# Attention maxima over 64 queries of two heads and 320 keys, with the attention's operands held in rings of chunks

## The chip, the cores and the metric

The kernel runs on one core of a Trainium2 chip. The metric is the device time of one execution in microseconds. The core's engines work side by side: TensorE (PE in the profile, its weight loads PEld) multiplies, VectorE (DVE), ScalarE (ACT) and GpSimd (POOL) do elementwise work, and SyncE (SP) issues the transfers (DMAs). Each engine executes its own instructions in a fixed order, and semaphores hold an instruction until what it needs is there.

## The reference

A gated mix of sliding-window attention and a two-layer gelu network, all in float32, over 2048 tokens of width 512; the attention has 32 heads of 16, each query sees itself and the 255 keys before it, and the inner width of the network is 1792.

```
qkv = (x @ wqkv).reshape(B, S, 3, H, Dh)
scores = einsum("bhqd,bhkd->bhqk", q, k) * Dh ** -0.5
mask = (idx[:, None] - idx[None, :] >= 0) & (idx[:, None] - idx[None, :] < W)
p = softmax(where(mask, scores, -1e9))
a = einsum("bhqk,bhkd->bhqd", p, v) ... @ wo
b = gelu(x @ w1 + b1) @ w2 + b2
g = sigmoid((x * gate_w).sum(-1))
return g * a + (1 - g) * b
```

## The kernel before

**Arithmetic.** Dense products are made of three matmuls each (`mm3`, L89 to L92): every operand is split into a high and a low part, and high by high, high by low and low by high are added in PSUM. The scores carry the split in their contraction instead: for one head the 16 elements of `q` and `k` stand there with high and low parts, 48 rows in all, so that two heads fill 96 of the 128 partitions.

**Stages.** Four tiles of 512 tokens are projected first (`qkv`): `q`, `k` and `v` go out to DRAM as `SQ`, `SK` and `SV`. The attention then runs over 8 groups of four heads, and in each over 16 blocks of 128 keys: 128 units `u`. Four units of one group (512 tokens) are called a chunk here; there are 32. The network (`mlp`) and the last product with `wo` (`final`) are cut into pieces of a few matmuls and put between the attention's by `fill`, so that TensorE has dense work while the attention's other engines run.

**The attention.** For a unit the maxima come first, 8 units ahead of the rest (LEAD):
- `att_max` (L385): a matmul `sm` (L394) gives the scores of 128 queries of one head by 384 keys; a reduction on DVE (L399) adds the mask and puts the maxima into `M`. Four of these per unit, one for each head.
- `att_rows` (L405): once a chunk, the negated maxima in two parts are transposed on DVE (`tt`, L414) and copied by four casts on POOL (L419) into eight further rows (96 to 103) of `qs`. The matching rows of `ks` hold ones for their own head (`clear_k`), so that the next matmul subtracts the maximum by itself.
- `att_exp` (L425): a matmul `st` (L435) gives, for 64 keys of two heads, the scores of 320 queries, transposed; ACT takes the exponential into `pt` (L450), and POOL zeroes the two corners outside the window (L441, L444).
- `att_pvs` (L456): once a chunk the products with `vbuf` (L472) collect numerators and denominators in two PSUM tiles; ACT and DVE add them into `nd` (L493, L496), and it is stored as `ND` (L497). For every second group `att_norm` (L503) divides, by way of DRAM (`den`, `RD`, `num`, `rb`, `OT`).

**What holds the operands.** `ks` holds the 2048 keys of one group in the layout that `st` wants: 64 keys of head 0 beside 64 of head 1, with zeros in the other's rows. `sm` reads the same tile with a strided view (`of_head`). `qs` holds the queries for both. `load_k` (L348) and `att_load` (L367) fetch a chunk's keys and queries for a later unit, overwriting those of the group before.

**What sets the order.** The code is unrolled. On PE, ACT, DVE and POOL the order is the one in which the program emits instructions (`manual_schedule`): the main loop, L743 to L774, goes through the units, in each four times through the letters of ORDER (`m` maxima, `s` exponentials, `p` products, `f` dense work of STEP = 2296 ns by the planner's count for a whole unit), and `after` puts follow-up work at a due time on a planner's clock. SP's order comes from the framework's own scheduler. SP issues every DMA of the kernel, in that order: one that waits holds all behind it. Each issue also waits until the DMA eight earlier has landed, since there are eight completion semaphores (DMAHW0 to DMAHW7 in the order).

## Time and profile before

| | us |
|---|---|
| median of 3 runs | 769.8 (769.8 to 769.93) |
| the profiled execution | 769.51 |
| its span, first to last instruction | 767.8 |
| granted TensorE clock, mean | 1.000 |

The profile is one execution. Busy times are sums over an engine's instructions; PE's matmuls overlap in the records, so the distance from start to start tells what one costs. A row of a group of instructions gives line, engine, operation, output and inputs with their shapes, count, busy time, mean ns of one, and the idle time just before them with what ended it. SPq is SP's issuing of DMAs. The page's rows by fortieths of the span show the load of TensorE and of the DMA engines in tenths:

```profile
PE   8999999988999999999999999999999999999998
DMA  9986856765643565575345756653575474436583
```

The first 160 us are projections, with heavy traffic to DRAM; from about 185 to 689 us the attention and the network run side by side; the last 80 us are the network's end and the product with `wo`.

### The profile page before, as it was taken

To read this page: it belongs to the slowest core of one execution; us is meant where nothing else is said; L and a number is where in the kernel's file an instruction comes from. 1 tells how busy PE (TensorE), PEld (TensorE's weight loads), DVE (VectorE), ACT (ScalarE), POOL (GpSimd) and SP (SyncE) were. 2 spreads that over 40 slices of the span, in tenths; PEclk is the share of its full clock that TensorE was granted. 3 is DMA by queue.
4 is the path that set the end of the run, shared out by engine and by line. 5 is a ranking of instruction groups with operands and counts; after the bars stand their busy time and mean duration, and the time that the engine had idled before them with its cause. 6 is when DMAs were issued, how large, how long until landed. Compare 5 with 4: busy or idle time off the path is not lost.

```text
span 767.8 us, 18330 instructions
## 1 busy us (share of the span) xinstructions
PE 748.8 (98%) x6102; PEld 614.3 (80%) x6102; DVE 534.1 (70%) x1548; ACT 432.6 (56%) x945; POOL 385.9 (50%) x1125
## 2 busy tenths in 40 slices
PE   8999999988999999999999999999999999999998
PEld 6888888866888888788877877888888788878786
DVE  4532332889669868976897798679878886893553
ACT  4434433358458646754885587448646763785641
POOL 2200000018666765766567677658765775777200
PEclk9999999999999999999999999999999999999999
DMA  9986856765643565575345756653575474436583
GB/s 299 358 296 203 319 182 219 252 195 166 179 119 73 181 196 138 142 209 151 95 114 156 212 163 193 185 126 94 172 206 158 107 214 125 132 107 200 171 261 110
DMA packets 136558, 137.81 MB, mean 179 GB/s; under 512 B 53264, under 2 KB 88592, under 8 KB 136464
## 3 DMA queue, kind: packets, MB, share of 16 engines
q1 hardware_dynamic: 136464, 136.64, 59.4%
q8 instruction: 49, 0.80, 0.4%
q14 instruction: 45, 0.37, 0.2%
HBM read 82.58 MB, written 54.00 MB: 178 GB/s over the span
## 4 chain that ended last, share of the span: by engine, by line
PE 84%; DVE 8%; issue 3%; ACT 3%; DMA 1%; SPq 1%; POOL 0%; DVEq 0%; POOLq 0%; ACTq 0%
PE sm L394 10%; PE st L435 8%; PE pv_sm L472 7%; PE y L90 7%; PE y L91 6%; PE y L92 6%; PE u L90 5%; PE u L91 5%; PE u L92 5%; PE qk L92 4%; DVE jm L399 4%; PE qk L90 4%; PE qk L91 4%; PE a L90 2%; PE v L92 2%
## 5 line engine op out<-in xcount | busy, mean ns | idle before, releaser
L399 DVE CUSTOM_DVE_ANT_0 jm<-sm,mask 128x384 bf16<-128x384 f32 (+2 forms) x512 | 269.6, 527 | 66.8 <-PE sm L394 38.8
L450 ACT ACTIVATE pt<-st 128x320 f32<-128x320 f32 (+4 forms) x512 | 206.1, 421 | 134.1 <-PE st L435 129.4
L441 POOL TENSOR_SCALAR_AFFINE_SELECT pt<-pt 64x128 f32<-64x128 f32 x512 | 176.5, 345 | 184.8 <-ACT pt L450 166.1
L394 PE MATMUL sm<-ks,qs 96*128 96x384 f32 (+2 forms) x512 | 171.7, 338 | 10.7 <-DVE M L399 9.0
L435 PE MATMUL st<-qs,ks 128*128 128x320 f32 (+4 forms) x512 | 155.0, 305 | 0.7 <-ACT pt L450 0.7
L444 POOL TENSOR_SCALAR_AFFINE_SELECT pt<-pt 64x128 f32<-64x128 f32 x448 | 154.7, 345 | 0.0
L394 PEld LDWEIGHTS sm<-ks,qs 96*128 96x128 f32 x512 | 96.2, 188 | 44.1 <-DVE M L399 21.1
L435 PEld LDWEIGHTS st<-qs,ks 128*128 128x128 f32 x512 | 97.3, 190 | 18.3 <-ACT pt L450 1.1
L90 PE MATMUL y<-w,h 128*128 128x512 f32 x224 | 90.1, 402 | 0.0
L91 PE MATMUL y<-w,h 128*128 128x512 f32 x224 | 88.4, 395 | 0.0
L92 PE MATMUL y<-w,h 128*128 128x512 f32 x224 | 87.8, 392 | 0.0
L419 POOL CAST qs<-tt 8x256 fp32r<-8x256 f32 x128 | 62.3, 487 | 47.2 <-PE u L92 37.9
L90 PE MATMUL u<-mx,w 128*128 128x512 f32 x196 | 80.4, 410 | 0.0
L91 PE MATMUL u<-mx,w 128*128 128x512 f32 x196 | 77.3, 395 | 0.0
L92 PE MATMUL u<-mx,w 128*128 128x512 f32 x196 | 76.8, 392 | 0.0
L472 PE MATMUL pv_st<-pt,vbuf 64*32 64x320 f32 (+4 forms) x1408 | 73.1, 346 | 0.8 <-POOL pt L441 0.8
L472 PE MATMUL pv_sm<-pt,vbuf 64*32 64x320 f32 (+4 forms) x1408 | 73.4, 346 | 0.1
L472 PEld LDWEIGHTS pv_sm<-pt,vbuf 64*32 64x32 f32 x1408 | 49.9, 106 | 19.9 <-issue 2.1
L251 DVE TENSOR_TENSOR qke<-qk,qke 128x512 fp32r<-128x512 f32 x32 | 22.1, 690 | 48.9 <-ACT qke L248 40.5
L248 ACT ACTIVATE qke<-qk 128x512 fp32r<-128x512 f32 x32 | 19.1, 598 | 56.0 <-PE qk L92 37.1
L92 PEld LDWEIGHTS y<-w,h 128*128 128x128 f32 x224 | 42.1, 188 | 9.7
L496 DVE TENSOR_TENSOR nd<-nd,pv_sm 128x512 f32<-128x512 f32 x32 | 21.9, 684 | 39.0 <-ACT nd L493 38.8
(124 smaller groups left out, 1337.6 us busy)
## 6 DMA issues: line engine op xcount, KB each, us to landing
mx<-XT SPq DMA_DIRECT2D x24, 512.0 KB
SQ<-qke SPq DMA_DIRECT2D x16, 512.0 KB
SK<-qke SPq DMA_DIRECT2D x16, 512.0 KB
qs<-SQ SPq DMA_DIRECT2D x32, 256.0 KB
ND<-nd SPq DMA_DIRECT2D x32, 256.0 KB
ks<-SK SPq DMA_DIRECT2D x112, 64.0 KB
raw_w<-in_B_w_dram SPq DMA_DIRECT2D x28, 256.0 KB
SV<-vx SPq DMA_DIRECT2D x16, 272.0 KB
```

The source lines that it names most:

```text
L90: nc.tensor.matmul(p, lh, rh, start=first, stop=False)
L91: nc.tensor.matmul(p, lh, rl, start=False, stop=False)
L92: nc.tensor.matmul(p, ll, rh, start=False, stop=last)
L251: nc.vector.tensor_sub(e[:, 1 - h], p, f32(e[:, h]))
L394: nc.tensor.matmul(p[:, :w], qs[0:96, pr, b * 128:(b + 1) * 128], of_head(ks[0:96, pr, 2 * k0:2 * (k0 + w)], s), start=True, stop=True)
L399: nc.vector.tensor_tensor_reduce(junk[:, :w], p[:, :w], mask[:, 384 - w:384], 1.0, -3e38, ALU.add, ALU.max, M[:, b % RB, i:i + 1])
L419: nc.gpsimd.tensor_copy(dst, tt[32 * i:32 * i + 8].unsqueeze(1).broadcast_to([8, 2, RB, 32]))
L435: nc.tensor.matmul(p[:, :w], ks[:, pr, 2 * k0:2 * k0 + 128], qs[:, pr, k0:k0 + w], start=True, stop=True)
L441: nc.gpsimd.affine_select(out=v[:, :, 0:64], in_=v[:, :, 0:64], pattern=[[0, 2], [1, 64]], compare_op=ALU.is_ge, fill=0.0, base=0, channel ...
L444: nc.gpsimd.affine_select(out=v[:, :, W:W + 64], in_=v[:, :, W:W + 64], pattern=[[0, 2], [-1, 64]], compare_op=ALU.is_ge, fill=0.0, base=- ...
L450: nc.scalar.activation(pt[:, pr, :w], p[:, :w], AF.Exp, scale=SCALE)
L472: nc.tensor.matmul(pv[r // 64][32 * i:32 * i + 32, q - c * T:e - c * T], vts[g_, b // NB][r:r + 64, v:v + 32], rhs(r), start=start, stop=s ...
```

## The change

The maxima get operands of their own, and all of the attention's operands are held by chunks.

- **`sm`** now takes 64 queries of both heads (128 columns of `qd`, 64 of one head beside 64 of the other) by 320 keys (`kd`). The mask has 320 columns, with one 64 by 64 corner pair in each half of the partitions. There are still four `sm` per unit: two halves of the block by two pairs of heads.
- **Heads.** A group is two heads out of each of two 128-wide pieces of the projection, so `SQ` and `SK` in DRAM are laid out by piece, and `SK` is cut into four tiles of 512 tokens.
- **Rings.** `ks`, `qd` and `kd` each have two slots of one chunk; `kd` holds 256 earlier keys besides the 512 (the halo). The slot is the parity of the chunk's number. `qs` keeps all 2048 queries; the rows for the maxima are now 0 to 3 and 64 to 67.
- **Loads.** A chunk takes 6 DMAs for `ks`, 4 for `kd` (2 in a group's first chunk), 4 for `qd` and 4 for `qs`, against 7 to 10 for `ks` and 2 for `qs` before. They are emitted at fixed units: `qd` and `kd` when the maxima begin a chunk, `ks` one unit later, `qs` two units later. SP issues 1029 DMAs in all, 841 before.
- **Maxima's rows.** The transpose is 256 columns wide instead of 128, and each of the four casts writes 4 rows of 2 x 256 elements instead of 8 rows of 2 x 128.
- **Memory.** `pt` has 14 buffers instead of 16, `h` 7 instead of 8, `raw` 2 instead of 3 (early weights use `pt` buffers). The `v` eviction has four pieces instead of two; `wo` comes in four DMAs a block, in the new order of heads; the network's results for the last stage are fetched into `qd` and `kd` instead of `ks`.

```diff
-    SK = dr.tile([H, 16, 2, S], F32, name="SK")
+    SK = [dr.tile([H // NC, 16, 2, NC, T], F32, name=f"SK{t}") for t in range(NT)]
...
-    ks = cp.tile([128, 2, 2 * S], F32R, name="ks")
+    ks = cp.tile([128, 2, 2, 2 * T], F32R, name="ks")
+    qd = cp.tile([128, 2, 2, 2 * T], F32R, name="qd")
+    kd = cp.tile([128, 2, 2, W + T], F32R, name="kd")
...
-            to = vx[:, :, 0:16].rearrange("p (g s a) d -> p g a s d", s=2, a=2)
-            for s in range(2):
+            to = vx[:, :, 0:16].rearrange("p (i g s a) d -> p i s g a d", i=2, s=2, a=2)
...
+    def slot(g_, c):
+        return (g_ * NT + c) % 2
...
+    def parts(st, g_, h):
+
+        for s in range(2):
+            src = heads(st, g_)[s]
+            yield s, 0, 32, src.rearrange("d u a c -> (d u) a c")
+            yield s, 32, 16, src[:, h]
+
+    def load_ks(g_, c):
...
+        for s, r, n, src in parts(SK[c], g_, 0):
+            r += 64 * s + 4
+            v = f32(ks[r:r + n, slot(g_, c)]).rearrange("r a (n u j) -> r (a n) u j", u=4, j=64)
+            src = src.rearrange("r a (n u j) -> r (a n) u j", u=2, j=64)
+            if s:
+                nc.sync.dma_start(v[:, :, 0], src[:, :, 0])
+                nc.sync.dma_start(v[:, :, 3], src[:, :, 1])
+            else:
+                nc.sync.dma_start(v[:, :, 1:3], src)
+
+    def load_kd(g_, c):
+        for t in range(max(c - 1, 0), c + 1):
+            ready(t, g_, 1)
+            k0 = 0 if t == c else T - W
+            at = W if t == c else 0
+            src = heads(SK[t], g_)[:, :, :, :, k0:]
+            to = f32(kd[:, slot(g_, c), :, at:at + T - k0])
+            nc.sync.dma_start(to[0:64], src.rearrange("s d u a c -> (s d u) a c"))
+            nc.sync.dma_start(to[64:96], src[:, :, 0].rearrange("s d a c -> (s d) a c"))
+
+    def load_qd(g_, c):
...
+        for s, r, n, src in parts(SQ[c], g_, 1):
+            r = r * 2 + n * s
+            v = f32(qd[r:r + n, slot(g_, c)]).rearrange("r a (n s j) -> r (a n) s j", s=2, j=64)[:, :, s]
+            nc.sync.dma_start(v, src.rearrange("r a (n j) -> r (a n) j", j=64))
...
-        w = (b + 1) * 128 - k0
-        pr, s = divmod(i, 2)
...
-        nc.tensor.matmul(p[:, :w], qs[0:96, pr, b * 128:(b + 1) * 128], of_head(ks[0:96, pr, 2 * k0:2 * (k0 + w)], s),
+        hb, pr = divmod(i, 2)
+        c, n = b // NB, slot(g_, b // NB)
+        j = 2 * (b % NB) + hb
+        w = min(64 * (2 * b + hb + 1), W + 64)
+        k1 = 64 * (j + 1) + W
+        p = ps.tile([128, 320], F32, tag="sm", bufs=3, name=f"sm{g_}_{b}_{i}")
+        nc.tensor.matmul(p[:, :w], qd[0:96, n, pr, 128 * j:128 * (j + 1)], kd[0:96, n, pr, k1 - w:k1],
...
-            dst = qs[96:104, :, rb * RB * 128:(rb + 1) * RB * 128]
...
-            nc.gpsimd.tensor_copy(dst, tt[32 * i:32 * i + 8].unsqueeze(1).broadcast_to([8, 2, RB, 32]))
+            r = 64 * (i // 2)
+            dst = qs[r:r + 4, :, rb * RB * 128:(rb + 1) * RB * 128]
...
+            nc.gpsimd.tensor_copy(dst, tt[32 * i:32 * i + 4].unsqueeze(1).broadcast_to([4, 2, 2 * RB, 32]))
...
-        if m % NB == LPOS and m > 0 and chunks:
-            att_load(*chunks.pop(0))
+        if m in range(1, NT + 1):
+            load_qs(0, m - 1)
+        if m % NB == 0 and 0 < m < NU - NB:
+            load_qd(*divmod(m // NB + 1, NT)), load_kd(*divmod(m // NB + 1, NT))
+        if u % NB == 1 and NB < u < NU - NB:
+            load_ks(*divmod(u // NB + 1, NT))
+        if u % NB == 2 and NB < u < NU - 3 * NB:
+            load_qs(*divmod(u // NB + 3, NT))
...
-PTS = 16
+PTS = 14
+RAWS = 150e3
```

On TensorE, in the third unit of the first group, the order before reads as follows (`u` is the network's first product, `sm_10_3` the maxima of unit 10, `st_2_2` the scores of unit 2):

```order
L90 MATMUL u_6_1757<-xt_914,w_6_1460 128x512
L91 MATMUL u_6_1757<-xt_914,w_6_1460 128x512
L92 MATMUL u_6_1757<-xt_914,w_6_1460 128x512
L394 MATMUL sm_10_3_1785<-ks,qs 128x384
L435 MATMUL st_2_2_1790<-qs,ks 128x320
```

and now:

```order
L93 MATMUL u_6_1812<-xt_941,w_6_1525 128x512
L94 MATMUL u_6_1812<-xt_941,w_6_1525 128x512
L95 MATMUL u_6_1812<-xt_941,w_6_1525 128x512
L439 MATMUL sm_10_3_1837<-kd,qd 128x320
L482 MATMUL st_2_2_1843<-qs,ks 128x320
```

Nothing has moved on TensorE; `sm` reads `kd` and `qd` and is 64 columns narrower.

On SP, around the store of `nd` of the third group's second chunk, the order before reads (the names in brackets are what an issue waits for):

```order
L361 DMA ks<-SK 16x4x128 [waits DMAHW1_49]
L372 DMA qs<-SQ_71 64x2x512 [waits DMAHW2_49]
L373 DMA qs<-SQ_71 32x2x512 [waits DMAHW3_49]
L497 DMA ND_1_92<-nd_1_4620 128x512 [waits DMAHW4_49,DVE_49]
L380 DMA vbuf<-SV_77 128x4x34 [waits DMAHW5_49,PE_49]
L382 DMA vbuf<-SV_77 64x4x34 [waits DMAHW6_49]
L382 DMA vbuf<-SV_77 64x4x34 [waits DMAHW7_49]
L361 DMA ks<-SK 32x4x128 [waits DMAHW0_49,PE_49]
```

and now, first to the last of the `kd` loads:

```order
L410 DMA qd<-SQ_71 32x16x64 [waits DMAHW7_49,PE_49]
L544 DMA ND_1_95<-nd_1_4721 128x512 [waits DMAHW0_49,DVE_49]
L410 DMA qd<-SQ_71 16x16x64 [waits DMAHW1_49]
L410 DMA qd<-SQ_71 32x16x64 [waits DMAHW2_49]
L410 DMA qd<-SQ_71 16x16x64 [waits DMAHW3_49]
L402 DMA kd<-SK_74 64x2x256 [waits DMAHW4_49]
L403 DMA kd<-SK_74 32x2x256 [waits DMAHW5_49]
L402 DMA kd<-SK_75 64x2x512 [waits DMAHW6_49]
L403 DMA kd<-SK_75 32x2x512 [waits DMAHW7_49]
```

and behind these the `vbuf` and `ks` loads:

```order
L425 DMA vbuf<-SV_80 64x4x34 [waits DMAHW2_49]
L393 DMA ks<-SK_77 32x8x128 [waits DMAHW3_49]
L393 DMA ks<-SK_77 16x8x128 [waits DMAHW4_49]
L390 DMA ks<-SK_77 32x8x64 [waits DMAHW5_49]
L391 DMA ks<-SK_77 32x8x64 [waits DMAHW6_49]
L390 DMA ks<-SK_77 16x8x64 [waits DMAHW7_49]
L391 DMA ks<-SK_77 16x8x64 [waits DMAHW0_49]
```

Before, the last `ks` and `qs` loads of a later chunk stood ahead of this store and few loads behind it. Now three `qd`, four `kd`, three `vbuf` and six `ks` loads stand behind it, and the `ks` loads are those of the chunk whose scores come next.

On POOL, where a chunk's maxima go into `qs`, the order before reads (`pt` are the corners that POOL zeroes):

```order
L419 CAST qs<-tt_2_1896 8x2x4x32 x3
L441 AFFINE_SELECT pt_4_1_1909<-pt_4_1_1909 64x2x64
L444 AFFINE_SELECT pt_4_1_1909<-pt_4_1_1909 64x2x64
L441 AFFINE_SELECT pt_4_1_1909<-pt_4_1_1909 64x2x64
L444 AFFINE_SELECT pt_4_1_1909<-pt_4_1_1909 64x2x64
L419 CAST qs<-tt_2_1896 8x2x4x32
```

and now:

```order
L465 CAST qs<-tt_2_1951 4x2x8x32 x3
L488 AFFINE_SELECT pt_4_1_1964<-pt_4_1_1964 64x2x64
L491 AFFINE_SELECT pt_4_1_1964<-pt_4_1_1964 64x2x64
L488 AFFINE_SELECT pt_4_1_1964<-pt_4_1_1964 64x2x64
L491 AFFINE_SELECT pt_4_1_1964<-pt_4_1_1964 64x2x64
L465 CAST qs<-tt_2_1951 4x2x8x32
```

The casts stand where they stood, with half as many partitions and twice as many elements in each.

More of the change, by code (lines that the diff above doesn't have):

```diff
@@ L743, in gated_mix @@
     NU = NG * NKB
[L744 removed]
+    NQ = NG * NT
     fill(START - AHEAD)
     need(("v", NT - 2, NB - 1))
[L747 removed]
+    for c in (0, 1):
+        load_qd(0, c)
     fill(AHEAD)
```

139 lines of the change are left out of this document (70 added, 69 removed).

## The prediction

> **What bounds the kernel now.** I read the page's engine lines first, then its chain, then one stretch of the timeline on TensorE.
>
> ```profile
> span 767.8 us, 18330 instructions
> PE 748.8 (98%) x6102; PEld 614.3 (80%) x6102; DVE 534.1 (70%) x1548; ACT 432.6 (56%) x945; POOL 385.9 (50%) x1125
> ...
> PE 84%; DVE 8%; issue 3%; ACT 3%; DMA 1%; SPq 1%; POOL 0%; DVEq 0%; POOLq 0%; ACTq 0%
> ```
>
> ```profile
> 250.41 0.34 PE L394 MATMUL sm<-ks,qs 96*128 96x384 f32 x1
> 250.58 0.31 PE L435 MATMUL st<-qs,ks 128*128 128x320 f32 x1
> 250.73 0.40 PE L90 MATMUL u<-mx,w 128*128 128x512 f32 x1
> 250.96 0.39 PE L91 MATMUL u<-mx,w 128*128 128x512 f32 x1
> ```
>
> Durations on TensorE overlap; what counts is the pitch from start to start: 0.17 us for 384 columns, 0.15 for 320, 0.23 for 512. So (0.23 - 0.15)/192 columns = 0.42 ns a column, and TensorE runs matmul behind matmul. The view by stretches gives the attention loop after its start-up:
>
> ```profile
> 185.00:689.00 504.00, 495.89 (x4694) 408.87 (x4693) 406.47 (x1263) 315.46 (x709) 337.24 (x988) 1.00 0.55 153
> 160.00:185.00 25.00, 20.58 (x91) 15.25 (x90) 21.62 (x60) 19.13 (x40) 13.82 (x32) 1.00 0.55 178
> ```
>
> (PE, PEld, DVE, ACT, POOL, then clock, DMA share, GB/s.) In 504 us TensorE idles 8.1 us, in the start-up 4.4. TensorE is the bound; DVE at 406 of 504 is next. These stretches hold 29 chunks of four key blocks, 504/29 = 17.4 us each.
>
> **The change, part by part.**
>
> TensorE and DVE. The order shows `sm` 64 columns narrower in unchanged places.
>
> ```profile
> L394 PE MATMUL sm<-ks,qs 96*128 96x384 f32 x448 | 155.5, 350 | 10.7 <-DVE M L399 9.0 <-DVE nd L496 1.2
> L399 DVE CUSTOM_DVE_ANT_0 jm<-sm,mask 128x384 bf16<-128x384 f32 x448 | 247.1, 551 | 54.3 <-PE sm L394 29.4 <-PE st L435 0.3
> L399 DVE CUSTOM_DVE_ANT_0 jm<-sm,mask 128x256 bf16<-128x256 f32 x32 | 13.6, 424 | 8.6 <-PE sm L394 7.1
> L414 DVE STREAM_TRANSPOSE tt<-nm x32: 310/311/315, 149.3 to 691.7; 128x128 f32<-128x128 f32 x32
> ```
>
> 448 matmuls lose 64 x 0.42 = 27 ns: 12.0 us. Of the 64 in blocks 0 and 1 half lose as much: 0.8. Together 12.8 us off TensorE, 0.43 a chunk; a chunk that nothing else holds goes from 17.4 to 16.95. DVE's reduction loses 64 x (551-424)/128 = 64 ns, 448 times 28 us, and the transpose of twice the width costs between 0 and 311 ns more (say 160 x 32 = 5 us). DVE is hidden behind TensorE, so what it gives is only TensorE's idle time before `sm`: between 0 and 8.1 + 4.4 us; I take 5, of which 1.5 in the start-up.
>
> POOL. Each of 128 casts writes 512 elements a row, not 256.
>
> ```profile
> L419 POOL CAST qs<-tt x128: 391/396/879, 149.7 to 696.1; 8x256 fp32r<-8x256 f32 x128
> ...
> 331.11 0.39 POOL L419 CAST qs<-tt 8x256 fp32r<-8x256 f32 x1
> ...
> 331.83 0.31 PE L435 MATMUL st<-qs,ks 128*128 128x320 f32 x1
> ```
>
> Between nothing and double, so up to 0.4 us each; I take 0.3, 38 us on POOL, whose 337 of 504 us leaves room. The rows are needed by an `st` two blocks on. The rows quoted are a tight chunk: the cast ends at 331.50, `st` starts at 331.83, 0.33 us of slack. A chunk with the fourth cast so late loses some tenths; bounds 0 and 31 x 0.4 = 12 us, I take 1.
>
> DMA engines. Per chunk the new issues carry 2304 pieces of 256 B, 384 of 512 B, 144 of 1 KB and 384 of 2 KB (partitions times pieces in the order's shapes), 3216 against 960, and 1.72 MB against 0.79: over 32 chunks 72,000 packets and 30 MB more.
>
> ```profile
> DMA packets 136558, 137.81 MB, mean 179 GB/s; under 512 B 53264, under 2 KB 88592, under 8 KB 136464
> q1 hardware_dynamic: 136464, 136.64, 59.4%
> ```
>
> By bytes that is 59.4% x 30/136.6 = 13% more of the span, by packets 59.4% x 72/136 = 31%. Both leave the 16 engines below 100%, so bandwidth costs nothing by itself, but landings get longer. The Trainium skill ("DMA: Bandwidth & Descriptors", Specifications) says that transfers under 512 B are read-modify-write; by it the sum would be DMA-bound, rival (4). The row speaks against it: at twice an average packet's time the 53,264 packets under 512 B would take 53,264/136,464 x 2 x 59.4% = 46% of the span, and leave 13%, 100 us, for the over 100 MB of the rest, above 1 TB/s.
>
> SyncE, the place that decides. All DMAs are issued by SP in order. Before, `ks` holds all 2048 keys, and a chunk's keys are loaded far ahead. Now `ks` is a ring of two chunks: a slot is free when its chunk's last `st` has run, at the start of the chunk before the one that needs it, and all six `ks` DMAs must land before that chunk's first `st`. In the order they stand behind the store of `nd`, which waits for that chunk's PV, and behind three `qd`, four `kd` and three `vbuf` issues. The rows of one chunk before, on TensorE, ACT, DVE and SP:
>
> ```profile
> 339.44 0.37 PE L435 MATMUL st<-qs,ks 128*128 128x320 f32 x1
> 343.76 0.27 PE L472 MATMUL pv_sm<-pt,vbuf 64*32 64x128 f32 x1
> 344.12 0.60 ACT L493 ACTIVATE nd<-pv_st 128x512 f32<-128x512 f32 x1 [1.88 <-PE pv_sm L472]
> 344.75 0.69 DVE L496 TENSOR_TENSOR nd<-nd,pv_sm 128x512 f32<-128x512 f32 x1 [1.96 <-ACT nd L493]
> 347.21 0.37 SPq L497 DMA_DIRECT2D ND<-nd  x1
> 347.68 0.38 SPq L380 DMA_DIRECT2D vbuf<-SV  x1
> 348.11 1.30 SPq L382 DMA_DIRECT2D vbuf<-SV  x2
> 354.85 2.73 SPq L361 DMA_DIRECT2D ks<-SK  x6
> 356.55 0.31 PE L435 MATMUL st<-qs,ks 128*128 128x320 f32 x1
> ```
>
> ```profile
> 309.65 0.62 SPq L372 DMA_DIRECT2D qs<-SQ  x1
> 310.32 0.59 SPq L373 DMA_DIRECT2D qs<-SQ  x1
> ...
> 747.86 0.33 SPq L551 DMA_DIRECT2D or<-OT  x1
> ...
> 750.70 0.63 ACT L554 ACTIVATE ot<-or 128x512 fp32r<-128x512 f32 x1 [3.59 <-DMA or<-OT]
> ```
>
> `nd` is ready at 345.44, 6.0 us after the chunk's first `st`. One issue costs 2.73/6 = 0.46 us (`ks` rows) to 0.65 (`qs` rows, start to start). From the last row pair a load lands 750.70 - 748.19 = 2.5 us after its issue. The new shapes lie between these prices: I put `qd` and `ks` at 0.46 (nearest: short pieces into strided rows) and `kd` at 0.62 (nearest: `qs`). Then ND 0.47, `qd` 3 x 0.46, `kd` 4 x 0.62, `vbuf` 1.78 (347.68 to 349.41 and a gap), `ks` 6 x 0.46 make 8.9 us. The keys are there 6.0 + 8.9 + 2.5 = 17.4 us after the chunk began; TensorE would want them after 17.1 - 0.43 = 16.7. So `ks` arrives some 0.7 us late and the whole in-order TensorE waits, `sm`, dense work and all.
>
> The order has three kinds of such chunks, counted from ND to the last `ks`: 10 with 15 or 16 issues, or with no more cost (loads of chunk 0 have no halo), about 8.2 us; 10 with 16 to 18, about 9.2; 9 with 19 to 22 (`ya` loads, weights, `mx` between), about 10.4. With 8.5 around them: 16.7, 17.7, 18.9. The first kind stays with TensorE at 16.95. Sum: 169.5 + 177 + 170 = 516.6 against 504, a loss of 12.6 us. Less 1.5 in the start-up, less 2.5 of DVE stalls in the first kind, plus 1 for the casts: the span goes to about 777.5, and the time, which lies 2.0 above the span (769.8 against 767.8; the profiled execution itself 769.51), to 779.5. With all new issues at 0.46 and landing 0.3 sooner, the three kinds are 16.95, 16.95 and 17.8: 499, so 762. With all at 0.65 and a landing of 3 us they are near 18.4, 19.8 and 21: 571, so 835; but then the sum of issues passes what SP did in any stretch, so I cut there.
>
> The rest costs nothing, as long as its cover holds: `pt` with 14 buffers (12 tiles of six blocks live until the PV plus the two being written), seven `h` tiles (the eighth was only ahead), four evictions for two in the QKV stage on ACT (56% busy), `wo` in four pieces, `clear_q`. With two `raw` buffers SP waits for the weight splits more often:
>
> ```profile
> SPq L361 <- PE st L435: 65.7, 53, 6.1
> SPq L137 <- DVE w L149: 24.6, 16, 4.1
> SPq L497 <- DVE nd L496: 23.8, 13, 4.5
> ```
>
> These waits fall into the 14 loads in chunks 10 to 15, which are of the late kinds already. The first row is SP being ahead of TensorE by up to 6 us: this is the slack that the ring takes away.
>
> **Rivals.** (1) SP keeps up: issues cost 0.46 throughout, `nd` comes earlier because DVE is lighter, and the keys land in the shadow of the chunk. Then TensorE's 12.8 us and 3 to 7 of its stalls come back: 769.8 - 12.8 - 4 = 753. For it: the `ks` rows at 0.46, a chunk is only 0.7 us short; it decides as soon as ND to the last `ks` takes under 8.2 us. Against it: `kd` copies the shape of the `qs` rows, and nine chunks are 1 to 2 us over. (2) In part: all new issues at 0.46 and the landing 0.3 sooner, the lower case of the sum, where only the nine longest chunks lose: 762. For it: the `ks` rows; against: the `qs` pair at 0.65. (3) SP as a whole is the bound: chunks that also carry `den`, `RD`, `num`, `rb`, `OT` have 30 to 33 issues of 0.5 us, 16 us and their waits, so backlog carries over: 1 us more in 16 chunks, 796. For it: the 23.8 us of waits on `nd`; against: half of the chunks have 24 to 27 issues and let it drain. (4) Each new packet takes two average ones' time on the engines: 2 x 72/136 x 59.4% = 63% of the span more, 122% with what is there, so the whole is DMA-bound at 1.22 x 768 = 935. This is the page's rule above. Against it stand the 46% just worked out. (5) The casts late in every chunk: 12 us more than nothing on the TensorE-bound time, 765 alone, hidden when the keys are later.
>
> **How the numbers follow.** Forecast (SP-issued keys late in most chunks, 768 to 792) 48%, centre 779; (1) 19%; (2) 12%; (3) 16%; (4) 1%; (5) 4%. The predicted time is 779. The range for 8 in 10 takes in rival (2), most of (1) and (3): 755 to 802; the likeliest case's own is 768 to 792. About 0.2%, 1.5 us, is what this measurement can tell from no change. Faster: (1), (2) and most of (5), 32%; within: 6%; slower: the rest, 62%.
>
> **What would show it.** Right: waits of PE on a DMA `ks<-SK` at the first `st` of a chunk, 0.5 to 2 us each, 20 or so of them; PE's busy share in 185 to 689 falls below 495.9/504; SP issues back to back from ND to the last `ks`; the `sm` pitch 0.15 us; `jm` near 488 ns. Wrong: no PE wait on `ks`, and chunks of 16.5 to 17 us; or waits of PE on POOL's casts, or a DMA share near 1.00. A `kd` issue at 0.46 us would shift the sum by 0.6 us a chunk, a landing of 3.5 by 1.

## The result and the profile after

The changed kernel takes 860.48 us (median of 4 runs, 857.85 to 867.37) against 769.8 us: a ratio of 1.1192, with an interval of 1.1121 to 1.1263. The direction and the place were forecast, the size was not: 91 us lost where 9 were expected. Some executions fall into a slower state; among the runs below only the slowest of e17 (814.8 us) did, and its ratio leaves it out.

The profiled execution took 857.85 us. Its page, first the engines, then the DMA queue and the chain of waits:

```profile
span 856.1 us, 18480 instructions
PE 766.8 (90%) x6102; PEld 623.2 (73%) x6102; DVE 510.9 (60%) x1548; ACT 434.4 (51%) x973; POOL 422.2 (49%) x1129
...
DMA packets 213039, 167.71 MB, mean 196 GB/s; under 512 B 128464, under 2 KB 156880, under 8 KB 212944
...
q1 hardware_dynamic: 212944, 166.53, 70.7%
...
PE 62%; DMA 18%; SPq 10%; DVE 4%; issue 3%; ACT 2%; POOL 1%; DVEq 0%; POOLq 0%
```

TensorE still has the most work, but the chain runs on it for 62% of the span instead of 84%. DMA and SP's queue took 28% of the chain; they had 2%. TensorE idles 856.1 - 766.8 = 89 us, before 19: 70 of the 88 us between the two spans. The other 18 are in its busy time, which rose from 748.8 to 766.8 although each `sm` is narrower. The view by stretches (PE, PEld, DVE, ACT, POOL, clock, DMA share, GB/s) shows both:

```profile
160.00:185.00 25.00, 20.30 (x87) 16.98 (x86) 19.73 (x58) 17.94 (x38) 12.73 (x27) 0.86 0.60 132
185.00:771.00 586.00, 511.43 (x4691) 414.40 (x4691) 385.38 (x1262) 315.85 (x708) 370.50 (x989) 0.94 0.70 180
```

The granted clock, 1.00 before in every stretch, is 0.94 over the attention loop. The loop, 504 us before for about as many matmuls, took 586, and TensorE was busy in 511 of them, before in 496.

The waits, as engine, line, releaser, total, times and longest:

```profile
PE st L482 <- DMA ks<-SK: 54.4, 18, 8.0
...
DVE den L558 <- DMA den<-ND: 34.3, 13, 5.5
...
DVE num L568 <- DMA rb<-RD: 13.8, 8, 3.6
```

The first row is the wait that was forecast; it had no counterpart before. The other two were not forecast: DVE, in its fixed order, stands before the normalisation's small loads, and the maxima's reductions stand behind it. One chunk, on TensorE, ACT, DVE and SP:

```profile
402.06 0.38 PE L482 MATMUL st<-qs,ks 128*128 128x320 f32 x1 [1.69 <-DMA ks<-SK]
406.83 0.60 ACT L540 ACTIVATE nd<-pv_st 128x512 f32<-128x512 f32 x1 [0.40 <-PE pv_sm L519]
407.57 0.68 DVE L543 TENSOR_TENSOR nd<-nd,pv_sm 128x512 f32<-128x512 f32 x1
408.66 0.48 SPq L544 DMA_DIRECT2D ND<-nd  x1
409.19 1.52 SPq L410 DMA_DIRECT2D qd<-SQ  x3
412.64 1.64 SPq L403 DMA_DIRECT2D kd<-SK  x1
416.73 1.00 SPq L393 DMA_DIRECT2D ks<-SK  x2
419.23 0.43 SPq L391 DMA_DIRECT2D ks<-SK  x1
422.01 0.38 PE L482 MATMUL st<-qs,ks 128*128 128x320 f32 x1 [2.78 <-DMA ks<-SK]
```

It goes as the prediction put it: `nd` is ready 6.2 us after the chunk's first `st`, SP issues from the store to the last `ks` without a pause, the keys land 2.35 us after their last issue, and the next chunk begins in that moment. But from the store to the end of the last `ks` issue it took 11.0 us, where this kind of chunk was put at 9.2, and one `kd` issue took 1.64 us. Over the 28 chunks from the third to the thirtieth (chunk lengths here are distances between the first `st` of chunks, landings are the semaphore's last step in the trace), the mean is: `nd` ready at 6.80 us, its store issued 0.44 later, 10.91 to the end of the last `ks` issue, 2.19 to the landing; the chunks last 20.24. In 27 of the 28 the first `st` starts no later than 0.2 us after the keys' landing (on the mean 0.1 us ahead of that last step, at most 0.5).

What such a wait does to TensorE's clock, in the first late chunk:

```profile
201.67 0.39 PE L94 MATMUL y<-w,h 128*128 128x512 f32 x1
201.90 0.40 PE L95 MATMUL y<-w,h 128*128 128x512 f32 x1
206.32 0.39 PE L439 MATMUL sm<-kd,qd 96*128 96x64 f32 x1 [4.02 <-DMA ks<-SK]
208.75 0.60 PE L482 MATMUL st<-qs,ks 128*128 128x320 f32 x1 [2.04 <-DMA ks<-SK]
209.16 0.63 PE L93 MATMUL y<-w,h 128*128 128x512 f32 x1
209.58 0.63 PE L94 MATMUL y<-w,h 128*128 128x512 f32 x1
210.01 0.63 PE L95 MATMUL y<-w,h 128*128 128x512 f32 x1
```

Ahead of the wait 512 columns go by in 0.23 us, behind it in 0.42. The Trainium skill ("TensorE: Matmul & The Clock Gate", Part 1: The HAM clock gate) says that the array runs at half clock after an idle window of about 3.4 us, until about as long a busy one has passed. These rows agree: 0.42 against 0.23 is half speed, after 6 us nearly idle. In other chunks of this trace a shorter wait was enough: the granted clock fell to 0.50 behind single waits of 2.3 to 2.8 us too.

### The profile page after: what moved, and what is told of

It reads as the page before. It is cut to its first block, busy times and chain, and to the rows that moved or that the text cites. A ratio compares the mean times of both kernels' runs of the same rounds, so it can differ in the third digit from the quotient of the medians.

```text
span 856.1 us, 18480 instructions
## 1 busy us (share of the span) xinstructions
PE 766.8 (90%) x6102; PEld 623.2 (73%) x6102; DVE 510.9 (60%) x1548; ACT 434.4 (51%) x973; POOL 422.2 (49%) x1129
## 3 DMA queue, kind: packets, MB, share of 16 engines
q1 hardware_dynamic: 212944, 166.53, 70.7%
## 4 chain that ended last, share of the span: by engine, by line
PE 62%; DMA 18%; SPq 10%; DVE 4%; issue 3%; ACT 2%; POOL 1%; DVEq 0%; POOLq 0%
PE pv_sm L519 7%; PE st L482 6%; DMA ks<-SK 6%; PE sm L439 5%; PE u L93 4%; PE u L94 4%; PE u L95 4%; PE qk L95 3%; PE qk L93 3%; PE y L93 3%; PE qk L94 3%; PE y L94 3%; PE y L95 3%; DMA kd<-SK 3%; DVE jm L444 2%
## 5 line engine op out<-in xcount | busy, mean ns | idle before, releaser
L444 DVE CUSTOM_DVE_ANT_0 jm<-sm,mask 128x320 bf16<-128x320 f32 (+4 forms) x512 | 237.7, 464 | 122.5 <-PE sm L439 98.0
L488 POOL TENSOR_SCALAR_AFFINE_SELECT pt<-pt 64x128 f32<-64x128 f32 x512 | 184.2, 360 | 231.7 <-ACT pt L497 211.0
L482 PE MATMUL st<-qs,ks 128*128 128x320 f32 (+4 forms) x512 | 162.3, 320 | 59.7 <-DMA ks<-SK 54.4
L439 PE MATMUL sm<-kd,qd 96*128 96x320 f32 (+4 forms) x512 | 158.8, 313 | 16.7 <-DVE M L444 5.0
L491 POOL TENSOR_SCALAR_AFFINE_SELECT pt<-pt 64x128 f32<-64x128 f32 x448 | 154.0, 344 | 0.0
L439 PEld LDWEIGHTS sm<-kd,qd 96*128 96x128 f32 x512 | 99.7, 195 | 43.7 <-DVE M L444 12.1
L465 POOL CAST qs<-tt 4x512 fp32r<-4x512 f32 x128 | 90.6, 708 | 46.5 <-DVE tt L459 39.2
L95 PE MATMUL y<-w,h 128*128 128x512 f32 x224 | 90.6, 404 | 1.9 <-DVE h L634 1.9
L93 PE MATMUL y<-w,h 128*128 128x512 f32 x224 | 92.2, 412 | 0.0
L94 PE MATMUL y<-w,h 128*128 128x512 f32 x224 | 90.7, 405 | 0.0
L519 PE MATMUL pv_sm<-pt,vbuf 64*32 64x320 f32 (+4 forms) x1408 | 82.7, 378 | 1.1 <-DVE M L444 0.6
L519 PE MATMUL pv_st<-pt,vbuf 64*32 64x320 f32 (+4 forms) x1408 | 82.3, 378 | 0.5 <-POOL pt L488 0.5
L519 PEld LDWEIGHTS pv_st<-pt,vbuf 64*32 64x32 f32 x1408 | 50.2, 117 | 0.9 <-POOL pt L488 0.6
```

The costliest lines, as they stand in the source:

```text
L93: nc.tensor.matmul(p, lh, rh, start=first, stop=False)
L94: nc.tensor.matmul(p, lh, rl, start=False, stop=False)
L95: nc.tensor.matmul(p, ll, rh, start=False, stop=last)
L439: nc.tensor.matmul(p[:, :w], qd[0:96, n, pr, 128 * j:128 * (j + 1)], kd[0:96, n, pr, k1 - w:k1], start=True, stop=True)
L444: nc.vector.tensor_tensor_reduce(junk[:, :w], p[:, :w], mask[:, 320 - w:320], 1.0, -3e38, ALU.add, ALU.max, M[:, 2 * (b % RB) + hb, pr:pr ...
L465: nc.gpsimd.tensor_copy(dst, tt[32 * i:32 * i + 4].unsqueeze(1).broadcast_to([4, 2, 2 * RB, 32]))
```

## The experiments

All times are medians, beside the kernel before on the same chip (770.1 to 770.6 us). "SP" is the mean number of issues a chunk and their mean duration, counted in the trace from the second chunk's first `st` to the thirtieth's. Clock, SP and chunk are those of the profiled execution, which for e3 took 776.5 us and for e17 800.8.

| run | us | ratio, interval | clock | SP a chunk | mean chunk, us |
|---|---|---|---|---|---|
| before | 769.8 | | 1.000 | 21.2 x 0.480 | 17.3 |
| changed | 860.5 | 1.119, 1.112 to 1.126 | 0.952 | 27.3 x 0.506 | 20.2 |
| e1 ks a chunk early | 1063.0 | 1.378, 1.371 to 1.384 | 0.865 | 27.2 x 0.486 | 27.2 |
| e2 nd stored by ACT | 851.1 | 1.102, 1.098 to 1.107 | 0.947 | 26.3 x 0.507 | 20.3 |
| e3 no qd and kd loads | 772.4 | 1.003, 1.001 to 1.006 | 0.987 | 19.5 x 0.486 | 17.3 |
| e4 ks by ACT | 956.4 | 1.242, 1.238 to 1.246 | 0.917 | 21.2 x 0.484 | 23.7 |
| e5 ks at slot's release | 819.3 | 1.062, 1.060 to 1.065 | 0.971 | 27.2 x 0.519 | 19.0 |
| e6 tiny qd, kd | 844.3 | 1.096, 1.093 to 1.100 | 0.957 | 27.3 x 0.509 | 19.7 |
| e7 merged qd, kd | 824.1 | 1.070, 1.067 to 1.073 | 0.960 | 22.5 x 0.500 | 19.0 |
| e8 zeros ahead of st | 853.0 | 1.106, 1.104 to 1.108 | 0.982 | 27.3 x 0.504 | 20.0 |
| e9 all rings at release | 836.6 | 1.087, 1.081 to 1.092 | 0.953 | 27.3 x 0.518 | 19.6 |
| e10 and normalisation later | 817.6 | 1.062, 1.060 to 1.064 | 0.977 | 27.2 x 0.504 | 18.8 |
| e11 ks at release, norm. later | 822.9 | 1.070, 1.066 to 1.074 | 0.969 | 27.3 x 0.501 | 19.0 |
| e12 before + 8 issues | 796.9 | 1.034, 1.032 to 1.036 | 0.987 | 28.5 x 0.476 | 18.3 |
| e13 e10, last step later yet | 823.5 | 1.069, 1.066 to 1.072 | 0.975 | 27.2 x 0.501 | 18.8 |
| e14 e5 with tiny qd, kd | 805.6 | 1.046, 1.043 to 1.050 | 0.979 | 27.0 x 0.526 | 18.5 |
| e15 e14, normalisation later | 813.8 | 1.057, 1.052 to 1.062 | 0.969 | 27.1 x 0.515 | 18.7 |
| e16 e12, normalisation later | 817.0 | 1.060, 1.056 to 1.064 | 0.981 | 28.5 x 0.472 | 18.7 |
| e17 e5, DVE not in norm. | 807.7 | 1.045, 1.039 to 1.052 | 0.972 | 27.3 x 0.520 | 18.4 |
| e18 e5, qs and qd by ACT | 935.7 | 1.213, 1.210 to 1.216 | 0.929 | 19.3 x 0.496 | 22.4 |

**The first four: is it the place of the `ks` loads in SP's order?** e1 asks for the `ks` loads two units earlier (its expectation says one) and with priority:

```diff
-        if u % NB == 1 and NB < u < NU - NB:
-            load_ks(*divmod(u // NB + 1, NT))
+        if u % NB == 3 and u < NU - NB - 1 and u > 0:
+            with tc.high_priority():
+                load_ks(*divmod(u // NB + 2, NT))
```

> Only SP's order changes: the six ks loads are asked for one unit earlier and with priority, so they stand behind the nd store and two qd loads, and kd and vbuf behind them. Theory A (the keys of st land late because SP issues them behind the nd store and ten other loads): ks land about 6.8 + 0.4 + 1.1 + 3.0 + 2.7 = 14 us into a chunk, the waits of st on ks go, and kd, now last, lands at about 17 us and takes over some waits in the chunks with many issues: 775 to 800 us, and the granted clock returns to 0.98 or more. Theory B (SP is saturated over the whole chunk, whatever the order): the lateness moves from ks to kd in every chunk, 840 to 860. Theory C (the lower granted clock is a cost of its own, not a consequence of stalls): clock still near 0.95 and at least 800 us.

1063 us. The framework's scheduler put the loads a whole chunk early, ahead of the release of their slot, and SP stood there:

```profile
SPq L393 <- PE st L482: 137.7, 30, 10.2
SPq L390 <- PE st L482: 97.6, 16, 7.3
```

So it did not test what it was to test. It shows the price of a wait at the head of this queue: up to 10 us at a time, in a queue of 27 issues a chunk.

e2 takes the store of `nd` off SP:

```diff
-            nc.sync.dma_start(ND[c][g_ // 2][g_ % 2], nd)
+            nc.scalar.dma_start(ND[c][g_ // 2][g_ % 2], nd)
```

> Only the store of nd moves, from SP's queue to ACT's; SP no longer waits for nd. Theory A: qd, kd, vbuf and ks are issued from about 1 us into a chunk on, 14 to 16 issues of 0.55 us, ks land at about 12 us, st no longer waits: TensorE-bound, 757 to 770 us, less a stall of some 0.7 us a chunk on ACT that waits for nd. Theory B (SP saturated): 28 issues of 0.55 us are 15.4 of 17 us with other waits beside, so the ks still arrive late in the longest chunks: 790 to 830. Theory C: clock stays at 0.95, at least 800 us.

851 us, and the keys were as late as ever (20.3 us a chunk). SP did not get ahead:

```profile
SPq L423 <- DMA ND<-nd: 20.2, 7, 5.4
SPq L425 <- DMA ND<-nd: 17.5, 7, 4.2
```

Eight completion semaphores go round over the DMAs of both queues: in the trace the 32 stores that ACT issues stand on the same eight as SP's loads. SP's `vbuf` issues now waited for the landing of a store that ACT had not been able to issue. The wait for `nd` is still in SP's line, by way of a semaphore.

e3 leaves out the loads of `qd` and `kd` after the third chunk:

```diff
-        if m % NB == 0 and 0 < m < NU - NB:
+        if 0 < m < NB + 1 and m % NB == 0:
```

> The loads of qd and kd are left out after the third chunk, so the maxima of later chunks are of old keys and queries; all else as in the changed kernel. Eight issues a chunk fewer stand between the nd store and the last ks. Theory A: ks land 4.5 to 5 us earlier, about 15 us into a chunk, and the chunk is TensorE-bound at about 17 us: 755 to 765 us, granted clock 1.00. If nd and the landing are late for another reason than the issues ahead, chunks stay over 18 us: 790 and more.

772.4 us: 88 of the 91 us are back. Without these 7.5 issues a chunk, the keys land 2.5 us before they are needed on the mean, and only three of 28 chunks start with them. In two stretches without weights and late normalisation:

```profile
185.00:300.00 115.00, 114.72 (x1128) 95.75 (x1126) 85.27 (x294) 70.32 (x159) 86.39 (x244) 1.00 0.56 158
500.00:600.00 100.00, 99.71 (x991) 83.04 (x990) 76.18 (x256) 62.35 (x142) 73.13 (x199) 1.00 0.55 149
```

TensorE is full, at full clock, and these chunks take 16.0 to 17.1 us: the narrower `sm` does shorten a chunk that nothing holds. The loss comes back in the chunks with weights and normalisation (up to 22.5 us), and in the start and end around the attention, which are 4 and 7.5 us longer than before (in an execution 4 us over this run's median).

e4 issues the six `ks` loads on ACT (`nc.scalar.dma_start` in `load_ks`), at the release of their slot.

> The six ks loads are issued by ACT, as soon as the slot's last st has been issued; SP keeps the rest. Theory A: ks land within 8 us of a chunk's start, kd at about 14 us, and nothing of SP is late: TensorE-bound, 752 to 765 us, with ACT busier by 6 x 0.45 us a chunk. Theory B: 23 issues left on SP fit as well, so 755 to 765 too; this run tells A and B together from C (clock 0.95 and at least 800 us) and from a rival D, that issues on ACT delay the exponentials: then st waits on ACT, 780 or more.

956 us. Theories A and B did not allow it; rival D's "780 or more" did, but `st` hardly waits on ACT (5.6 us in 3 waits). ACT itself stands before its `ks` issues, SP behind the landing of those loads: the semaphores couple both queues, now in both directions:

```profile
ACT pt L497 <- DMA ks<-SK: 70.5, 21, 6.7
...
SPq L423 <- DMA ks<-SK: 88.0, 12, 9.4
```

**The next four: place, issues, traffic or clock.** e5 does what e1 was to do, by emitting the loads earlier without priority (e1's edit without the `with` line). They then stand ahead of the next `nd` store.

> The ks loads of a chunk are emitted two units earlier, at the last st of the chunk that frees their slot. In SP's order they now stand directly ahead of the nd store, behind the loads of the chunk before; all other loads keep their places. Theory A (ks late because of its place behind the nd store and ten loads): ks issued 0.3 to 3.5 us into a chunk and landed by 7, no waits of st on ks; the nd store at 6 us as before, kd landed by 14 us, in time; chunks of 16.0 to 17 us, granted clock 0.99 or more: 755 to 768 us. Theory B (SP has more issues than a chunk holds): 29 issues of 0.52 us and two waits (for st, for nd) pass 17 us, lateness moves to kd: waits of sm on kd, 790 to 840. Theory C (the clock falls by itself): clock about 0.95, 800 or more.

819 us. The `ks` landed 10 us before they were needed on the mean, and no chunk waited for them; that gives back 41 us. But chunks were still 19.0 us on the mean: 16.0 to 17.1 us where nothing else was to do, and 18 to 25 in those with normalisation, weights or `mx`. There, DVE waits:

```profile
DVE num L568 <- DMA rb<-RD: 28.6, 10, 5.3
DVE den L558 <- DMA den<-ND: 13.9, 7, 3.6
```

One of these waits, on DVE and then on TensorE:

```profile
313.78 0.69 DVE L568 TENSOR_TENSOR num<-num,rb 128x512 f32<-128x512 f32 x1 [4.52 <-issue]
...
314.94 0.41 PE L439 MATMUL sm<-kd,qd 96*128 96x320 f32 x1 [2.93 <-DVE M L444]
```

`num` is held for its loads (the view names `issue`; in the trace `rb` landed at 313.70), the reduction behind it is late, `sm` finds no free bank, and TensorE stops. In 15 of 29 chunks `kd` had landed only 0.1 to 0.5 us before its first `sm`. So theory A was half right: the place of `ks` costs 41 us, and then the next loads in the queue are the late ones, as theory B had it.

e6 keeps all issues and makes those of `qd` and `kd` one partition each; e7 keeps most of the bytes in some 3 issues a chunk instead of 7.5 (a line of e6 and two of e7):

```diff
+            v, src = (v[0:1], src[0:1]) if (g_, c) > (0, 2) else (v, src)
...
+            src = SQ[c][0:3, :, :, a0:a0 + 2].rearrange("h d u a c -> (h d u) a c")
+            nc.sync.dma_start(v, src.rearrange("r a (n j) -> r (a n) j", j=64))
```

> As the changed kernel, with the same issues of qd and kd in the same places, but each moves one partition instead of 16 to 64 (32 for the low parts), from the third chunk on, so the maxima of later chunks are of old data. Traffic as in the run without these loads, issues as in the changed kernel. Theory A (the number of issues): ks as late as in the changed kernel but for a landing some 0.5 us shorter: 835 to 860 us. Rival T (the traffic of qd and kd makes landings long and fills the engines): 770 to 785, as without the loads.

> As the changed kernel, with nearly the bytes of qd and kd in 3 issues instead of 8 (one qd load of 96 rows by 1024 elements with half the columns, two kd loads of 96 rows), so the maxima of later chunks are of other rows. Theory A: five issues of 0.6 us fewer, ks 3 us earlier, which is the mean lateness: 770 to 785 us. Rival T: 830 to 860.

e6: 844 us. The DMA share of its attention fell from 0.70 to 0.50:

```profile
185.00:755.00 570.00, 506.77 (x4696) 412.87 (x4695) 384.97 (x1263) 316.48 (x709) 372.04 (x992) 0.95 0.50 141
```

and that was worth 16 of the 91 us; the keys were late in 27 chunks again. Issues decide, traffic adds. e7: 824 us, so 36 us for the issues; more was expected. Its larger loads take longer to land, and SP waited 24.6 us for completion semaphores at the `ks` issues.

e8 puts 24 matmuls of zeros (bf16, 128 by 128) ahead of the first `st` of each chunk but the first:

```diff
+        if i == 0 and kb % NB == 0 and g_ + kb > 0:
+            for _ in range(WARMST):
+                nc.tensor.matmul(p[:, 0:128], zero, zero, start=True, stop=True)
```

> As the changed kernel, with 24 matmuls of zeros (128 by 128, bf16) ahead of each chunk's first st but the first, into the bank that st overwrites: some 2 to 3 us of work in TensorE's wait. Nothing else is changed. Theory A with the clock as a consequence of idle stretches: they fall into the wait for ks, so they cost little, TensorE is idle for less than 2 us at a time and the clock stays near 1.00; the PV and nd of late chunks come earlier, so 820 to 845 us. Theory C (the clock falls for another reason): clock 0.95 as before, and the time the same or up to 30 us longer (860 to 890).

853.0 us, between the two expectations: 7.5 less, with more work on TensorE. The clock rose from 0.952 to 0.982, and `nd` was ready at 6.23 us instead of 6.80. So the fall of the clock is a consequence of idle time, and the loop is: keys late, TensorE idle, clock halved, products and `nd` late, store late, keys late again. Most of the clock came back and 7.5 us with it, not the 18 by which busy time rose. Why so little was not tested; it fits that only the work up to `nd`, the first 6 to 7 us of a chunk, stands ahead of the store.

**The rest: what stays when `ks` is early.** e9 is e5 with `qd` and `kd` moved to the release of their slots too, e10 is e9 with the normalisation's steps due later, e11 is e5 with only these later steps:

```diff
-        if m % NB == 0 and 0 < m < NU - NB:
-            load_qd(*divmod(m // NB + 1, NT)), load_kd(*divmod(m // NB + 1, NT))
+        if m % NB == NB - 1 and m < NU - NB - 1:
+            load_qd(*divmod(m // NB + 2, NT)), load_kd(*divmod(m // NB + 2, NT))
...
-        after(6000, rcp), after(10500, back), after(17000, mul)
+        after(9000, rcp), after(15000, back), after(24000, mul)
```

> As the run with ks loaded when its slot is free (819.3 us), and the loads of qd and kd moved likewise: they are emitted when the last sm has read their slot, so that all 14 ring loads stand ahead of the nd store. In that run kd landed 0.1 to 0.5 us before its first sm in 11 of 29 chunks, and DVE waited 28.6 us for rb and 13.9 for den. Theory A2 (SP is late in three places: ks, kd, and the small loads of the normalisation, for which DVE holds the maxima's reductions): kd is in time, the waits for rb and den stay: 785 to 805 us. Theory B2 (what is left of the loss is traffic, DMA share 0.78 and issues stretched by it): 810 to 825.

> The run before, and DVE's and SP's steps of the normalisation are due later (9, 15 and 24 us in place of 6, 10.5 and 17), so that DVE meets loads that have landed. Theory A2: no wait of TensorE on SP's loads is left but in the chunks with weights; chunks of 16.0 to 17 us, clock 0.99: 755 to 772 us. Theory B2: 800 to 820.

> As the run with ks loaded when its slot is free, with only the later steps of the normalisation; kd stays behind the nd store. Theory A2: the waits of DVE on rb and den go, those of sm on kd stay: 785 to 805 us. Theory B2: 810 to 825. Together with the two runs above it gives each place its share.

836.6, 817.6 and 822.9 us: none went under e5 by more than 2 us. e9 brings the ring loads in time in all but two chunks, and the `nd` store, now behind them, is issued 5.3 us after `nd` is ready (0.44 in the changed kernel); the waits of DVE on `rb` grow from 28.6 to 52.2 us. e10 has them back at 38.2. Each of these orders has its late load.

e12 turns the question round: the kernel before, with eight idle loads of 1 KB a chunk.

```diff
+            for k in range(8):
+                nc.sync.dma_start(extra[:, k], SQ[0][k, :, 0, 0:16])
```

> The kernel before, with eight further loads of 16 rows by 64 bytes a chunk into a tile that nobody reads, issued at the place of the vbuf loads: SP issues as many DMAs a chunk as in the changed kernel, without its traffic and without the rings. Theory A2 (issues cost only where a ring leaves no slack): SP's stretches of waiting for a free slot in ks shrink, the normalisation is late by up to 4.5 us in a few chunks: 770 to 778 us. Rival S (SP's number of issues alone is the loss): 800 or more.

796.9 us, between the two expectations and close to rival S's 800: 27 us for eight issues that move next to nothing and that nobody waits for. From its view of waits, and the stretch of its attention:

```profile
DVE den L512 <- DMA den<-ND: 19.8, 8, 5.7
```

```profile
185.00:689.00 504.00, 480.96 (x4509) 398.36 (x4508) 381.99 (x1195) 293.44 (x659) 314.26 (x935) 0.98 0.53 146
```

No ring is here, and the DMA share is that of the kernel before (0.53 against 0.55). What is late is the normalisation, in the chunks that carry it: the five longest take 21.5 to 23.5 us, while 18 of the 28 stay at 16.3 to 17.9.

e14 is e5 with the tiny loads of e6. e13, e15 and e16 are e10, e14 and e12 with the normalisation's steps due after 9, 15 and 31 us (6, 10.5 and 17 in e14 and e12; 9, 15 and 24 in e10), to take DVE's wait away.

> As the run with all ring loads at the slot's release and the normalisation later (817.6 us), with its last step on DVE due after 31 us instead of 24, 16 us after num and rb are asked for. Theory N (the rest is DVE waiting for rb, 38 us there, and with it the maxima and TensorE): those waits go, 775 to 795 us. Theory T2 (the rest is traffic: landings of 5 to 9 us make all loads late in turn): 805 to 820.

> As the run with ks loaded when its slot is free (819.3 us), and the loads of qd and kd move one partition each, so the maxima of later chunks are of old data; all issues stay. Theory N: kd still counts as late only by its issue, the waits of DVE on rb and den stay: 800 to 815 us. Theory T2: landings of 2.3 us as in the changed kernel with tiny loads: 772 to 788.

> The run before with the normalisation's steps due after 9, 15 and 31 us. All three are away: the place of the ks loads, the traffic, and DVE's wait; the number of issues stays. Both theories: 758 to 775 us. If it stays above 785, the number of issues itself holds something that none of the three names.

> The kernel before with eight idle issues a chunk (796.9 us), and the normalisation's steps due after 9, 15 and 31 us. Theory N: all of the 27 us were DVE waiting for den and rb: 769 to 776 us. If other loads are late by the issues (vbuf, qs): 785 to 797.

e14 gave 805.6, so the traffic is worth 14 us here too. The other three were slower than the runs they build on, by 6, 8 and 20 us. DVE's waits on `rb` are gone from them (38.2 us in e10, 20.8 in e14; e12 had 0.2), but those on `den` grew, to 30.0, 30.5 and 29.2 us (2.2, 12.8 and 19.8 before). And `num` and `rb` hold two of the three `tmp` buffers for longer, which the next `nd` needs: ACT's `nd` waited 10.1 us for the store of `num` in e13 and 17.2 in e15; in e16 only 0.7, so there the cause stays open. They settle nothing about the normalisation's share.

e17 leaves DVE's two steps of it out and keeps the DMAs:

```diff
-            nc.vector.reciprocal(den, den)
-            nc.sync.dma_start(RD[t][c].rearrange("h (j c) -> (h j) c", c=32), den)
+            nc.sync.dma_start(RD[t][c].rearrange("h (j c) -> (h j) c", c=32), one)
...
-            nc.vector.tensor_mul(num, num, rb)
```

> As the run with ks loaded when its slot is free (819.3 us). The normalisation keeps its DMAs, but its two DVE steps (reciprocal, product) are left out, so the heads' outputs are not divided and RD holds ones; DVE waits for none of its loads. Theory N (DVE held by late den, num and rb, 47 us of waits there): 780 to 795 us; sm's waits on kd stay. Theory T2 (traffic and kd alone): 812 to 820.

807.7 us, between its expectations. By the ratios (1.045 against 1.062) that is some 13 us under e5, give or take 5. DVE waits for no load there, and `kd` takes its place. The longest wait, on SP and then on TensorE:

```profile
447.19 0.98 SPq L395 DMA_DIRECT2D ks<-SK  x2
...
449.68 0.43 SPq L393 DMA_DIRECT2D ks<-SK  x1
450.65 0.35 SPq L147 DMA_DIRECT2D raw_w<-in_B_w_dram  x1
451.04 1.04 SPq L565 DMA_DIRECT2D num<-ND  x1
452.12 0.58 SPq L565 DMA_DIRECT2D rb<-RD  x1
452.81 0.40 SPq L546 DMA_DIRECT2D ND<-nd  x1
453.25 2.60 SPq L412 DMA_DIRECT2D qd<-SQ  x4
455.89 1.67 SPq L404 DMA_DIRECT2D kd<-SK  x1
...
459.97 0.59 SPq L405 DMA_DIRECT2D kd<-SK  x1
```

```profile
464.13 0.60 PE L441 MATMUL sm<-kd,qd 96*128 96x320 f32 x1 [5.74 <-DMA vbuf<-SV]
```

`nd` was ready 5.3 us after this chunk's first `st` at 442.30, at 447.64; its store was issued at 452.81, since SP was still busy with what stood ahead of it. `kd`, behind the store, landed 0.35 us before `sm` started. (The wait is put down to `vbuf`, which landed near the same time; `sm` reads `kd` and `qd`.) SP worked almost without a gap for the whole chunk and was 5 us behind.

e18 keeps every load and takes eight issues a chunk off SP, by issuing `qs` and `qd` on ACT.

> As the run with ks loaded when its slot is free, with the loads of qs and qd issued by ACT; nothing is left out. SP issues 19 a chunk, as in the run without qd and kd (772.4 us). Theory S (what SP issues in a chunk decides): kd at 11 us, den and rb in time: 768 to 785 us, if ACT with 8 x 0.5 us a chunk more is not late itself. Theory T2: DMA share stays at 0.78 and the time at 805 to 820. Rival D (ACT's issues wait for free slots and hold the exponentials): waits of PE and POOL on ACT, 830 or more.

935.7 us, as rival D said (830 or more), with the waits that it named:

```profile
PE st L482 <- ACT pt L497: 110.3, 37, 8.2
...
ACT pt L497 <- DMA vbuf<-SV: 44.0, 7, 10.2
ACT pt L497 <- DMA qd<-SQ: 43.4, 9, 9.8
```

ACT stands before its issues until older DMAs of either queue have landed (`vbuf` is SP's, `qd` its own); the exponentials wait behind, and TensorE behind them. The Trainium skill ("DMA: Bandwidth & Descriptors", Issuing engines are not separate DMA queues) says that issuing from several engines saves only the time of the sequencer, "which is usually small relative to the DMA itself". For a single load the runs agree: a `ks` issue takes 0.52 us in the changed kernel, its landing 2.19 more. For a queue of such loads they do not: in e12 the issues of the eight idle loads, 8 x 0.45 us a chunk, cost 27 us. And in e2, e4 and e18 the time could not be saved, since the shared semaphores carried the waits across.

No run was faster than the kernel before.

## Why the prediction was wrong

- **TensorE.** Right in the pitch: `sm` has 0.15 us. The 16.95 us for an undisturbed chunk came out of a mean of 17.4 that holds the long chunks too. Undisturbed ones took 16.5 and 17.1 us in turn before; in e3 they take 16.1 and 17.0, 0.3 less where 0.43 was said.
- **DVE and POOL.** Right in size. These are the groups of the changed kernel:

```profile
L444 DVE CUSTOM_DVE_ANT_0 jm<-sm,mask 128x320 bf16<-128x320 f32 x448 | 217.2, 485 | 87.8 <-PE sm L439 65.5 <-DVE M L444 0.5
L459 DVE STREAM_TRANSPOSE tt<-nm 128x256 f32<-128x256 f32 x32 | 14.2, 445 | 3.7 <-POOL pt L491 0.5
L465 POOL CAST qs<-tt 4x512 fp32r<-4x512 f32 x128 | 90.6, 708 | 46.5 <-DVE tt L459 39.2
```

  A reduction takes 485 ns (487 worked out), the transpose 134 ns more (160 taken), a cast 708 on the mean against 487, 0.22 us more (0.3 taken). No wait of `st` is put down to a cast in the changed kernel, so rival (5) fell.
- **DMA engines.** Right in the load: 76,500 packets and 29.9 MB more (72,000 and 30), and 70.7% of the engines' time: not full. Rival (4) fell: by the queue's rows before and after, the new packets took 31 ns of an engine each, where the average one took 53 before and the rival took twice that, a factor of its own. Not right was "bandwidth costs nothing by itself": the traffic of `qd` and `kd` alone cost 16 us (e6) and 14 (e14).
- **Where TensorE would wait.** Right: at the first `st` of a chunk, on `ks<-SK`, 18 times in the view of waits ("20 or so" was said). But they were 3.0 us long on the mean and up to 8.0, where 0.5 to 2 was said, and by the landings 27 of 28 chunks were late, where the ten lightest were to stay with TensorE. So rivals (1) and (2) fell.
- **The sum on SP: the step that failed.** The path was the right one, its terms were too small: "6.0 + 8.9 + 2.5 = 17.4", with 8.2, 9.2 and 10.4 for the three kinds. The landing held (2.19 against 2.5). From the store to the last `ks` it took 10.91 us instead of 9.2: `qd` cost 0.60 from end to end instead of 0.46, `kd` 0.70 instead of 0.62, `ks` 0.52 instead of 0.46 (means, with 0.05 between), and another 0.7 us a chunk went to waits between issues. Some issues stretched to 1.8 us. `nd` was ready at 6.80 us instead of 6.0, and its store went out 0.44 later, for which the sum had nothing. Together 2.6 us a chunk, 73 us over 28 chunks; start and end of the kernel add 5 (185.57 us before the second chunk instead of 184.95, 69.5 behind the last one's first `st` instead of 64.9). That is the 78 us between the forecast of 779.5 and the profiled execution. The prices had been read off a few rows of the kernel before. The traffic is not what made the issues dearer on the whole: with loads of one partition (e6) one lasts 0.60 us (`qd`), 0.56 (`kd`) and 0.49 (`ks`), here 0.54, 0.64 and 0.48. What did was not tested.
- **What was missing in it.** The sum followed one path, from the `nd` store to the last `ks`, and let SP start each chunk with nothing left over. Over a whole chunk SP has 27.3 x (0.506 + 0.045) = 15.0 us of issues, before 21.2 x 0.525 = 11.1. It also waits for `nd` in line:

```profile
SPq L544 <- DVE nd L543: 62.1, 20, 7.8
```

  With the 13.7 us put down to `M` at the same line that is 2.7 us a chunk. 15.0 + 2.7 passes the 16.5 us that TensorE needs, so a chunk of that length has no room left even on the mean. That sum is an argument, not a measurement: over the 20.2 us that a chunk takes now SP is not full, it stands still for 5.2 of them. But counted by chunk, eight of the 28 hold 16.5 us of issues or more and last 22.4 us on the mean, the other twenty 19.4. So every chunk pays for the path above, and the fullest pay more. The latter is rival (3), which had 16% and was priced at 796 by an addition in 16 chunks. e12 shows that the issues alone can cost 27 us without any ring; that its 796.9 us is the rival's figure is chance, since the rival meant the whole change.
- **The range.** The upper case, 0.65 us an issue and 3 us of landing, gave 835 us and was cut because "the sum of issues passes what SP did in any stretch". It was the one place in the working where SP came near its limit, and it was read as a reason against the number.
- **The clock.** No step priced what follows a stall. e8, which brought most of the clock back, gained 7.5 us.

What is shown: the loss comes by SP's queue. Leaving out 7.5 issues and their traffic gives back 88 us (e3), the place of `ks` alone 41 (e5), 4.8 issues fewer with most of the traffic kept 36 (e7), traffic alone 14 to 16 (e6, e14), the clock about 8 (e8). These shares do not add up, as a load that is brought forward hands its lateness to the next. What stays open is how the 49 us that e5 keeps divide between `kd`, the normalisation and the weights: e17 puts some 13 on DVE's part of the normalisation, and e13, e15 and e16 brought waits of their own. No run gave the rings a third slot, which would let the loads come earlier, or merged the issues of a chunk with all of their data kept.

## What to carry to other kernels

Add up an in-order queue over the whole period of the loop, issues and waits together, and set the sum against the period of the engine that is the bound. Here the issues alone came to 15.0 of 16.5 us, and then reordering gave back 43 of the 91 us at best (e10) and chose which load was late next. A ring replaces slack that nobody counted: before it is put in, each load needs its earliest issue, its latest landing and its place in the queue. Price the second consequences of a stall too, here the slower clock and the in-order engines (DVE before `den` and `rb`) that stop other work.

## What the hardware showed unexpectedly

- Behind waits of 2.3 to 8 us TensorE's granted clock fell to 0.50 in 14 stretches of the attention loop, each 3.4 or 6.8 us long; over the loop that made 0.94.
- One DMA issue of the changed kernel's attention takes SP 0.43 us (`qs`) to 0.59 us (`kd`) as a median, but up to 1.8 us (`qd`, `kd`), and eight idle ones of 1 KB a chunk cost the kernel before 27 us.
- Moving issues from SP to ACT made the kernel slower in two runs of three (956 and 936 us, against 819 for e5, from which they differ in nothing else) and helped little in the third (851 against 860). In all three the queues of SP and ACT shared the eight completion semaphores.
